# Forget gates in 384-byte rows, joint decay sums and dummy matmuls in a tuned attention-and-feed-forward kernel

## The chip, the cores and the metric

The kernel runs on one core of one Trainium2 chip. The metric is device time in microseconds (us) for one launch, on that core. A run's span is the time from its first to its last instruction; the reported time is some 2 us longer. A run that is more than 1.5% above the fastest run of the same kernel is called slow, and ratios leave it out.

## The reference

The first layer is a gated linear attention with a state of 48 x 48 per head; the second is a feed-forward layer with the activation h + sin²(αh)/α.

```python
# q, k, v, f_logit: (4 batches, 8 heads, 768 tokens, 48)
f = 1.0 / (1.0 + np.exp(-f_logit))
for t in range(S):
    state = f[:, :, t, :, None] * state + np.einsum('bhd,bhe->bhde', k[:, :, t], v[:, :, t])
    y[:, :, t] = np.einsum('bhd,bhde->bhe', q[:, :, t], state)
x = y.transpose(0, 2, 1, 3).reshape(3072, 384)
h = x @ w_in                       # 384 x 2048
s = np.sin(alpha * h)
out = (h + s * s / (alpha + 1e-09)) @ w_out    # 2048 x 384
```

## The kernel before

Tokens are cut into six chunks of 128, and the four batches into two pairs. A pair in a chunk is a **unit**, so there are 12 units, and each needs one load of f, k, q and v (384 KB each). For a unit the kernel takes ln(1 + exp(-f)), sums it over the tokens of the chunk with a triangular mask on TensorE (the **decay sums**, tile `cs`), and multiplies q and k by exponentials of these sums.

A scheduler in the program places every operation. It works from hand-tuned tables of ranks and estimated durations; changing a table or a duration changes the order on every engine. The parts that the change touches:

```python
N_H, N_A, NQ, NV = 3, 3, 6, 4        # N_A: three PSUM banks shared by sums, transposes, scores, values
...
LOADS = [("v", 0), ("f", 0), ("q", 0), ("k", 0), ("f", 1), ("v", 1), ...]   # order in the load queue
W_GATE = [5, 5, 18]                  # w_in's two halves wait for load 5 (counted from 0), w_out for load 18
PHASES = [("pre", [0]), ("pre", [1]), ("sin", 16), ("pre", [2, 3]), ("sin", 16), ("pre", [4, 5]), ...]
...
def emit(e):                          # one load: 128 tokens on 128 partitions, rows of 48 floats (192 B)
    engine[e].dma_start(out=t, in_=srcs[n][bp * 2 * H:(bp + 1) * 2 * H, c * C:(c + 1) * C, :]
                        .rearrange("b c d -> c b d"))
...
def weights_after(i, rank):           # GpSimd reads one number of that load, then issues the weights' DMAs
    u, n = LOADS[W_GATE[i]][1], LOADS[W_GATE[i]][0]
    return op(rank, {POOL: 100}, lambda e: nc.gpsimd.tensor_copy(seen[:, i:i + 1], tl[n, u][0:1, 0, 0:1]), ...)
...
def cs_(e, i=i, m=m):                 # decay sums of ONE batch, in one bank
    cs = tl["cs", m] = ps_a.tile([P, 512], F32, tag="a", name=f"cs_{m}")
    nc.tensor.matmul(cs[:, :H * D]..., mask, lf_b[lf.place % 2][:, :, i, :, :D], start=True, stop=True)
    for p in range(0 if last else HP):
        nc.tensor.matmul(cs[:, H * D + p:H * D + p + 1], lf_b[...][:, p, i, :, :]..., ones_c, ...)
```

A phase `("pre", [2, 3])` runs the exponentials and logarithms of units 2 and 3 interleaved, under one function table of ScalarE; `("sin", 16)` runs sixteen sines under another, and each change of phase loads a table. Below, a **hidden product** is a matmul of x with w_in and an **output product** one with w_out; a **bank** is one of the parts of PSUM, where TensorE's results go; a **spread** is a 16 KB DMA that copies a part of x, transposed (xT), to other partitions.

## Time and profile before

| | before |
|---|---|
| time, median of 3 | 225.85 us (225.22 to 225.99) |
| span of the profiled run | 223.8 us |
| TensorE busy | 186.9 us (84%) |
| VectorE, ScalarE busy | 171.2 us, 160.9 us |
| mean granted TensorE clock | 0.954 |
| packets of the hardware load queue | 111,648 |

No engine is full over the whole span. TensorE is full in the second half and has gaps and a low clock in the first quarter; the prediction shows the slices and stretches from which this is read. ScalarE's table loads divide the front half into blocks, so they serve as milestones (start, length in us, engine, line, operation):

```profile
36.64 1.28 ACT L660 ACT_TABLE_LOAD   x1
45.68 1.28 ACT L660 ACT_TABLE_LOAD   x1
62.14 1.28 ACT L660 ACT_TABLE_LOAD   x1
```

The first sixteen sines end at 36.64; units 2 and 3 are prepared together until 45.68; the next sixteen sines end at 62.14.

### The profile page before, as it was taken

The numbers are of one execution on the slowest core, as the hardware profiler recorded it, in microseconds if no ns is written. First come the engines' busy times: TensorE is split into PE (matmuls) and PEld (weight loads), VectorE is DVE, ScalarE is ACT, GpSimd is POOL, SyncE is SP. The second block draws the span as 40 slices with busy tenths as digits, with TensorE's granted clock in tenths as the row PEclk, the third lists the DMA queues.
The fourth block names the chain that finished last, engine by engine and source line by source line (L and its number), as shares of the span: only waits on it lengthen the run. The fifth ranks groups of instructions, "written<-read, shape, count | busy, mean of one in ns | idle before, by whom it ended". The sixth has DMA issues, their size and how long they took to land.

```text
span 223.8 us, 4257 instructions
## 1 busy us (share of the span) xinstructions
PE 186.9 (84%) x1517; PEld 114.6 (51%) x1517; DVE 171.2 (76%) x306; ACT 160.9 (72%) x260; POOL 117.3 (52%) x142
## 2 busy tenths in 40 slices
PE   0266593848998999969698999988999999999993
PEld 0154382636864555636364655544655555555551
DVE  7769369497895699976997998678999767766730
ACT  2657269874699679978896879998976655688701
POOL 5037559077842696661364564679247778411300
PEclk9999589695899999979999999999999999999999
DMA  8999999995698999979999959966221020100121
GB/s 131 187 186 199 216 202 188 175 201 81 75 147 158 191 168 187 163 185 186 182 212 190 170 75 176 199 136 157 50 45 24 8 83 35 38 35 35 70 73 70
DMA packets 115125, 29.61 MB, mean 132 GB/s; under 512 B 108720, under 2 KB 114336, under 8 KB 115104
## 3 DMA queue, kind: packets, MB, share of 16 engines
q1 hardware_dynamic: 111648, 26.04, 67.4%
q0 software_dynamic: 3456, 3.30, 9.5%
q8 instruction: 12, 0.20, 0.4%
q14 instruction: 9, 0.07, 0.1%
HBM read 25.17 MB, written 4.72 MB: 134 GB/s over the span
## 4 chain that ended last, share of the span: by engine, by line
PE 54%; DVE 15%; ACT 9%; DMA 9%; POOL 5%; SPq 3%; issue 3%; ACTq 0%; POOLq 0%
PE h L549 24%; PE o L597 21%; DVE g L570 6%; SPq L277 3%; PE y L463 3%; DMA w_out_bf<-in_moe_w_out_dram 3%; DMA v<-in_v_dram 3%; DMA w_in_bf<-in_moe_w_in_dram 3%; DVE vb L348 3%; DVE vb L347 3%; ACT s L555 2%; ACT L660 2%; POOL qk L390 2%; DVE at L445 2%; PE aps L442 2%
## 5 line engine op out<-in xcount | busy, mean ns | idle before, releaser
L564 POOL TENSOR_TENSOR s<-s 128x512 f32<-128x512 f32 x63 | 65.5, 1050 | 46.9 <-ACT s L555 38.2
L555 ACT ACTIVATE s<-h,al_p 128x512 f32<-128x512 f32 (+1 forms) x112 | 66.3, 628 | 25.8 <-PE h L549 23.0
L549 PE MATMUL h<-xT,w_in_bf 128*128 128x512 bf16 (+1 forms) x336 | 79.5, 366 | 5.3 <-DMA w_in_bf<-in_moe_w_in_dram 3.4
L570 DVE SCALAR_TENSOR_TENSOR g<-s,al_r,h 128x512 bf16<-128x512 f32 (+1 forms) x112 | 71.1, 665 | 13.4 <-POOL s L564 11.1
L597 PE MATMUL o<-w_out_bf,g 128*128 128x384 bf16 x384 | 77.2, 331 | 2.6 <-DVE osb L605 1.3
L597 PEld LDWEIGHTS <-g 128*128 128x128 bf16 x384 | 36.5, 99 | 28.1 <-issue 3.2
L549 PEld LDWEIGHTS <-w_in_bf 128*128 128x128 bf16 x336 | 33.5, 103 | 29.2 <-DMA w_in_bf<-in_moe_w_in_dram 3.9
L445 DVE TENSOR_TENSOR at<-aps,mask 128x512 bf16<-128x512 f32 x48 | 31.3, 680 | 5.6 <-PE aps L442 5.4
L390 POOL TENSOR_TENSOR qk<-k,Gi 128x384 bf16<-128x384 f32 x20 | 20.5, 1042 | 23.5 <-ACT Gi L381 7.8
L463 PE MATMUL y<-at,vb 128*128 128x128 bf16 x184 | 18.5, 223 | 4.1 <-DVE at L445 2.3
L368 PE MATMUL cs<-lf,mask 128*128 128x384 bf16 x24 | 8.4, 358 | 13.7 <-ACT lf L341 13.5
L390 DVE TENSOR_TENSOR qk<-q,cs 128x384 bf16<-128x384 f32 x24 | 13.2, 549 | 6.9 <-ACT cs L377 6.7
L488 POOL TENSOR_TENSOR st<-sum,gl 128x512 bf16<-128x512 f32 x12 | 12.4, 1043 | 10.6 <-DVE sum L484 10.4
L562 ACT ACTIVATE s<-s 128x512 f32<-128x512 f32 x26 | 16.3, 631 | 0.5
L463 PEld LDWEIGHTS <-vb 128*128 128x128 bf16 x184 | 12.8, 100 | 6.3 <-issue 2.3
L381 ACT ACTIVATE Gi<-cs 128x384 f32<-128x384 f32 x24 | 11.7, 486 | 5.2 <-PE cs L371 5.0
L425 PE MATMUL tp<-ident,qk 128*128 128x128 bf16 x128 | 11.8, 246 | 4.0 <-POOL qk L390 3.5
L470 ACT CAST xT<-y 128x512 bf16<-128x512 f32 (+1 forms) x18 | 10.3, 580 | 6.2 <-PE y L463 5.1
L433 ACT COPY tr<-tp 128x1024 bf16<-128x1024 bf16 x10 | 10.1, 1010 | 6.4 <-PE tp L425 6.4
L660 ACT ACT_TABLE_LOAD x11 | 14.1, 1283 | 0.2
L338 ACT ACTIVATE f<-f 128x768 f32<-128x768 f32 x12 | 10.1, 838 | 5.0 <-DMA f<-in_f_logit_dram 4.9
L425 PEld LDWEIGHTS <-qk 128*128 128x128 bf16 x128 | 9.8, 113 | 6.2 <-POOL qk L390 4.0
(57 smaller groups left out, 178.7 us busy)
## 6 DMA issues: line engine op xcount, KB each, us to landing
v<-in_v_dram SPq DMA_DIRECT2D x12, 384.0 KB, 6.7
f<-in_f_logit_dram SPq DMA_DIRECT2D x12, 384.0 KB, 7.0
q<-in_q_dram SPq DMA_DIRECT2D x12, 384.0 KB, 6.6
k<-in_k_dram SPq DMA_DIRECT2D x12, 384.0 KB, 6.8
out_dram<-osb SPq DMA_DIRECT2D x24, 192.0 KB, 2.1
w_out_bf<-in_moe_w_out_dram POOLq DMA_DIRECT2D x4, 384.0 KB, 6.5
w_in_bf<-in_moe_w_in_dram POOLq DMA_DIRECT2D x8, 128.0 KB, 6.3
w_in_bf<-in_moe_w_in_dram POOLq DMA_DIRECT2D x4, 96.0 KB, 6.1
```

The source lines that it names most:

```text
L390: engine[e].tensor_mul(qk_b[bufs["qk", m].place % NQ][:, "kq".index(n), :, :, :D], tl[n, u][:, i * H:(i + 1) * H, :].rearrange("c (r p) d ...
L425: nc.tensor.transpose(tl[x, "tp"][:, j * HP + p, :], qk_b[qkb.place % NQ][:, j, p, :, :].rearrange("c r e -> c (r e)"), ident)
L445: nc.vector.tensor_mul(tl[x, "at", r], tl[x, "a"][r], mask4)
L463: nc.tensor.matmul(tl[x, "y"][:, blk, :], v_, tl[x, "at", r][:, p, :], start=(first and p == r == 0), stop=(r == 1), skip_group_check=True)
L488: engine[e].tensor_tensor(t, tl[x, "kv"] if c < SUM else tl[x, "sum"], tl["gl", m].unsqueeze(3).to_broadcast([P, HP, 2, E]), Alu.mult)
L549: nc.tensor.matmul(tl[x, "h"][:, part[i]], w_in_bf[:, kb, fbs[i] * P:(fbs[i] + 1) * P], tl["xT", c][:, kb, ts], start=(kb == 0), stop=(kb ...
L555: nc.scalar.activation(out=tl[x, "s"][:, part[i]], in_=tl[x, "h"][:, part[i]], func=Act.Sin, scale=al_p[:, fbs[i]:fbs[i] + 1])
L562: nc.scalar.activation(out=s2, in_=s, func=Act.Square)
L564: engine[e].tensor_mul(s2, s, s)
L570: nc.vector.scalar_tensor_tensor(tl["g", c, fb][:, ts], tl[x, "s2"][:, part[i]], al_r[:, fb:fb + 1], tl[x, "h"][:, part[i]], Alu.mult, Alu ...
L597: nc.tensor.matmul(tl["o", c, t], tl["g", c, fb][:, t * P:(t + 1) * P], w_out_bf[:, fb, :], start=(fb == 0), stop=(fb == FB - 1))
L660: nc.scalar.preload_act_table_set(now)
```

## The change

The intent: fewer and longer DMA rows for the forget gates, so that the saturated first 50 us carry less; fewer small operations on VectorE, by summing both batches of a unit together; dummy matmuls in TensorE's known gaps, so that its clock stays up. The tables are retuned for it.

```diff
+FILL = (12000, 60000)
-LOADS = [("v", 0), ("f", 0), ("q", 0), ("k", 0), ("f", 1), ("v", 1), ("q", 1), ("k", 1), ("v", 2),
+LOADS = [("f", 0), ("v", 1), ("k", 0), ("q", 0), ("q", 1), ("f", 1), ("v", 0), ("k", 1), ("f", 2),
+    ("f", 5), ("v", 3), ...
-W_GATE = [5, 5, 18]
+W_GATE = [7, 9, 17]
-PHASES = [("pre", [0]), ("pre", [1]), ("sin", 16), ("pre", [2, 3]), ("sin", 16), ("pre", [4, 5]), ...
+PHASES = [("pre", [0]), ("pre", [1]), ("sin", 16), ("pre", [2]), ("sin", 6), ("pre", [3]), ("sin", 10),
+    ("pre", [4, 5]), ...
  ... LAG, ATT, RANK, KIND, ON_ACT, BIAS: every number retuned (cut)
+            if n == "f":      # partition = a pair of tokens of one batch; 64 partitions per DMA
+                for i in range(2):
+                    engine[e].dma_start(out=t[i * E:(i + 1) * E].rearrange("c (h s) d -> c h (s d)", s=2),
+                                        in_=f_logit[2 * bp + i, :, c * C:(c + 1) * C, :]
+                                        .rearrange("h (c s) d -> c h (s d)", s=2))
+                return
-        o = bufs[n, u].ready = op(rank, {SP: 500}, emit, takes=[bufs[n, u]], dma=2100)
+        o = bufs[n, u].ready = op(rank, {SP: 1000 if n == "f" else 500}, emit, takes=[bufs[n, u]],
+                                   dma=1400 if n == "f" else 2100)
+        def cs_(e):           # both batches: two banks taken at once
+            cs = [ps_a.tile([P, 512], F32, tag="a", name=f"cs_{2 * u + i}") for i in range(2)]
+            warm(cs[0])
+            for s in range(2):
+                for i in range(2):      # batch i lies on 64 partitions, the other batch on the other 64
+                    nc.tensor.matmul(cs[i][...], maskf[i * E:(i + 1) * E, s, :],
+                                     lft[i * E:(i + 1) * E, :, s, :, :D], start=(s == 0), stop=(s == 1))
+            for p in range(0 if last else HP):
+                for s in range(2):
+                    nc.tensor.matmul(cs[0][:, H * D + 2 * p:H * D + 2 * p + 2], lft[:, p, s, :, :]...,
+                                     in_half, start=(s == 0), stop=(s == 1))
  ... one product gl per unit in place of two (cut)
+    def warm(t):              # dummies, before sums, transposes, scores and the first of a hidden block
+        for _ in range(gaps[0]):
+            nc.tensor.matmul(t, ident, mask4.rearrange("c p x -> c (p x)"), start=True, stop=True)
  ...
+        if e == PE:           # as many as fit in a gap that no bank limits
+            gap = o.start - max(pe_end, o.bank)
+            gaps[0] = max(0, int((gap - min(1500, 200 + gap // 4)) // 220)) if FILL[0] < o.start < FILL[1] else 0
+            pe_end = o.end
```

## The prediction

> **What bounds the kernel now.** I read the page first (busy shares and slices), then stretches of five and more microseconds, then TensorE's own timeline with its waits, and last the chain of waits. The busy shares name no engine: TensorE 84%, VectorE 76%, ScalarE 72%. The slices do: full speed and full occupancy in the second half, gaps and a low clock in the first quarter.
>
> ```profile
> PE   0266593848998999969698999988999999999993
> PEclk9999589695899999979999999999999999999999
> DMA  8999999995698999979999959966221020100121
> ```
>
> A slice is 5.6 us. Until 60 us TensorE is rarely full, and four slices have a clock of 0.5 to 0.8; DMA is saturated until 50 us. The same by stretches (columns: PE, PEld, DVE, ACT, POOL busy with counts, then clock, DMA share, GB/s):
>
> ```profile
> 20.00:25.00 5.00, 1.41 (x18) 0.83 (x14) 2.60 (x6) 3.26 (x4) 2.51 (x5) 0.80 1.17 211
> 25.00:30.00 5.00, 4.73 (x38) 3.75 (x39) 1.98 (x3) 2.27 (x5) 2.19 (x5) 0.52 1.15 211
> ...
> 35.00:40.00 5.00, 0.92 (x12) 0.63 (x11) 5.00 (x13) 4.94 (x9) 3.87 (x4) 1.00 1.34 188
> 40.00:45.00 5.00, 4.48 (x38) 3.18 (x34) 2.02 (x8) 4.19 (x9) 0.69 (x1) 0.66 1.21 175
> ...
> 50.00:55.00 5.00, 4.00 (x25) 3.01 (x26) 4.46 (x9) 1.58 (x4) 3.59 (x4) 0.53 0.75 104
> 55.00:60.00 5.00, 5.00 (x55) 4.12 (x54) 3.31 (x7) 3.53 (x8) 4.30 (x6) 0.79 0.27 29
> 60.00:125.00 65.00, 58.29 (x541) 35.91 (x540) 54.80 (x98) 54.48 (x85) 35.39 (x38) 0.97 1.09 176
> ```
>
> The reader is to see that each stretch of low clock follows one in which TensorE stood nearly idle (1.41 of 5, then 0.92 of 5, then 2.61 in 45 to 50). From 60 us on TensorE is 90% busy, 95% in 125 to 160 and 99% in 160 to 211: there its backlog sets the end. So what the front half saves counts as far as it lets TensorE start that backlog earlier. Its waits in the front, from its timeline (start, length, line, then the idle time before):
>
> ```profile
> 8.80 0.48 PE L368 MATMUL cs<-lf,mask 128*128 128x384 bf16 x1 [8.80 <-ACT lf L341]
> ...
> 12.47 1.03 PE L425 MATMUL tp<-ident,qk 128*128 128x128 bf16 x8 [2.37 <-POOL qk L390]
> ...
> 23.83 0.37 PE L549 MATMUL h<-xT,w_in_bf 128*128 128x256 bf16 x1 [2.38 <-DMA w_in_bf<-in_moe_w_in_dram]
> 25.25 0.39 PE L549 MATMUL h<-xT,w_in_bf 128*128 128x256 bf16 x1 [1.04 <-DMA w_in_bf<-in_moe_w_in_dram]
> ...
> 39.70 0.32 PE L368 MATMUL cs<-lf,mask 128*128 128x384 bf16 x1 [4.08 <-ACT lf L341]
> ```
>
> Two of the waits are for the decay sums' input (the first forget gates, and the exponentials that come after the sine block), one for the weights.
>
> **What the Trainium skill says.** (1) "TensorE: Matmul & The Clock Gate", section "What's actually happening": the clock halves after about one idle window of 3.4 us, and a busy window restores it. The trace agrees in size: three 128x256 matmuls take 0.64 us at 28.92 in the chain, while 21 of them take 2.61 us at 33.01, so 0.21 against 0.12 us each. (2) "DMA: Bandwidth & Descriptors", section "Specifications", puts line rate at pieces of 512 B and more. The trace shows 108720 of 115125 packets under 512 B and 187 to 211 GB/s when saturated; 384-byte pieces are still under that mark, so I expect a part of the gain, not a doubling of the rate. (3) "ScalarE: Activation LUTs", section "Step-by-step: what each stage is for", prices a table load at about 2.7 us with the drain; the trace has 1283 ns, which I use.
>
> **The change, part by part.**
>
> Forget gates. A load is now 2 DMAs with 1024 packets in all instead of one with 2048, so 12 loads save 12,288 packets. Loads follow each other every 2.05 us in the queue's view, 384 KB each. If the cost were all per packet, a load would take 1.03 us, if all per byte 2.05; I take 1.4 (an estimate; the scheduler's table in the diff also says 1400 for 2100). That is 0.65 us a load, 3.9 us for the six gates in the saturated first 50 us. The first gate is also now first in the queue. Before, the first v was issued at 0.82 and exp began at 7.03, which is two loads of 2.05 and a latency of about 2.1. With the new order: 0.82 + 1.4 + 2.1 = 4.3, so exp begins 2.7 us earlier. Then k (third) lands at 0.82 + 2.1 + 5.5 = 8.4 and q (fourth) at 10.5; k before, with four loads in front, at 11.1. With 0.55 us for the q product the first transposes run at about 11.3 instead of 12.47, the second gate's exp at about 14 instead of 15.73: about 1.5 us gained by then.
>
> Weights. The gate of w_in moves from the sixth load to the eighth (and, for the remaining half of its DMAs, to the tenth). Before, the gate opened at 15.54 and the last piece needed arrived at 25.25, 9.7 us later. The eighth load lands at about 18, the tenth at about 21 to 22; the four issues behind it take 2.1 us (0.52 each) and 5 us to land: about 28 to 29. So the first hidden matmul may be 3 us later. Against this, all attention of the first chunk but the last score product stands in front of it in the new order, so the sine block should run denser. I count this as 1 us lost net.
>
> Decay sums. 24 matmuls of 128 rows become 48 of 64 rows in alternating halves; 80 column sums stay 80. If the halves overlap, the 8.4 us stay; otherwise up to 24 x 0.16 = 3.8 us more at full clock, spread over the kernel. VectorE drops 10 products of 161 ns, 1.6 us. But a unit takes two of the three shared banks at once, and its first exponential waits for all 12 matmuls: about 0.5 us later per unit, mostly beside other ScalarE work. I count 0.5 us lost.
>
> Dummies. The built program has 21 of 128x512, 14 of them before one decay sum, the one that waited 4.08 us at 39.70. At 216 to 430 ns that block is 3 to 6 us inside a gap. In 20 to 60 us the low clock cost busy time times missing clock: 0.28 + 2.27 + 1.52 + 1.88 + 1.05 = 7.0 us of TensorE time. Only five dummies lie ahead of the hidden matmuls and two before the sums after, because elsewhere a bank limits the gap. I credit half, 3.5 us, and of that two thirds to the end, 2.3 us, since the chain in 25 to 60 us passes through VectorE (g, at and vb pieces) as well as TensorE.
>
> The schedule. Everything is retuned: two more table loads (2 x 1.28 = 2.6 us of ScalarE, as the second pre block is split), four PSUM copies of 1.01 us and four output copies less on ScalarE, which VectorE takes over at 0.69 and 0.55 us; all 30 spreads go to the sync queue, and three more loads now stand before its first wait for the spread. Before, that queue was blocked from 49.7 to 67.5 us while DMA fell to 29 GB/s. Two output tiles now run before the first chunk's hidden layer is done, 32 x 0.162 = 5.2 us of TensorE work put in its idle time. That is worth something only if VectorE, 96% busy in 80 to 100 us, follows. I credit 2.5 us, less 1 for the table loads.
>
> Sum: 1.5 + 2.3 + 1.5 - 1.0 - 0.5 = 3.8 us off 225.85; with some 0.7 us for the relief of DMA after 60 us (six gates of 0.65, mostly hidden), 4.5 us: 221.3.
>
> **Rivals.** First, weights bind: the second gate makes the first hidden matmul start at 29 and the whole sine block slides by 3 us or more, which eats the rest. For it speaks that the chain before passes through w_in; against it, that DMA has less to carry. Time 224 to 227. Second, VectorE takes over: it gets about 2 us more work and stands at 19.2 of 20 us in 80 to 100; then work saved ahead of 60 us becomes idle time of TensorE, and the time is 223 to 225. Third, the dummies and the earlier output matmuls keep the clock full through the front half and the retuned order closes the 12.6 us that TensorE idles after 60 us: all 7 us of clock and some of the idle time come back, 214 to 218. Fourth, two banks taken at once starve the attention: waits of transposes and scores for banks, 226 to 229; three banks with two claimed at once speak for it, the order tuned to that speaks against.
>
> **Range and chances.** 2% is 221.33 us, so my number lies on the border. The second rival and the third pull about equally; a retuned schedule is rarely slower than its predecessor, so slower by 2% (over 230.4) gets little. 80% range 215.5 to 225.8. Faster 0.48, same 0.46, slower 0.06.
>
> **What would show it.** Right: exp of the first gate begins at 4 to 5 us; packets of the hardware queue fall by some 12,000; clock slices below 0.8 shrink from four to one or two; TensorE's backlog phase starts with two output tiles done near 60 us. Wrong: first hidden matmul after 28 us with the sine block ending later than the 36.6 us of before; low clock in 40 to 60 still; more VectorE waits in 60 to 125, where TensorE would be under 58 of 65 us busy.

## The result, and the profile after

The changed kernel took **234.38 us** (median of 4 runs, one of them slow, 232.40 to 236.63), against 225.91 us of the kernel before in the same rounds. The ratio is **1.035** with a 95% interval of 1.025 to 1.046. (A ratio is the mean time of one kernel's fast runs over that of the other's of the same rounds, so it is not quite the ratio of the medians.) The result is right, the program is 3.5% slower, and the prediction was wrong in sign. The profiled run took 233.0 us with a span of 231.3.

A first ledger comes from the page. TensorE was busy 194.9 us and idle 231.3 - 194.9 = 36.4; before, busy 186.9 and idle 36.9. The dummies take 6.3 of the busy time. Time without useful work is therefore 36.4 + 6.3 = 42.7 against 36.9, so 5.8 us more, and useful work took 188.6 against 186.9, so 1.7 us more. The sum is the 7.5 us by which the span grew: TensorE mostly waits longer.

The slices of the changed kernel, 5.8 us each:

```profile
PE   0378469875898999859985998999999999999993
PEclk9999979999799999988996799999999999999999
DMA  6999999999990599977995992483402021100111
```

There are still four slices with a clock under 0.8, though milder ones (0.6 and 0.7; before 0.5, 0.6, 0.5 and 0.7), and they moved: two lie in the front, near 30 and 60 us, and two near 121 to 133 us, where before there was full speed. By stretches (busy us with counts of PE, PEld, DVE, ACT, POOL, then clock, DMA share, GB/s):

```profile
20.00:25.00 5.00, 4.20 (x46) 3.91 (x44) 3.37 (x8) 2.81 (x6) 4.19 (x10) 1.00 1.38 195
25.00:30.00 5.00, 1.45 (x15) 0.61 (x12) 2.51 (x4) 2.04 (x2) 2.40 (x6) 1.00 1.16 210
30.00:35.00 5.00, 3.98 (x28) 2.80 (x28) 2.72 (x5) 1.88 (x5) 2.93 (x5) 0.66 1.23 203
...
40.00:45.00 5.00, 3.84 (x28) 1.64 (x27) 4.62 (x12) 3.79 (x7) 2.69 (x3) 1.00 1.13 176
...
55.00:60.00 5.00, 1.94 (x17) 0.99 (x14) 1.19 (x3) 4.38 (x10) 3.02 (x4) 0.81 1.25 182
60.00:125.00 65.00, 56.66 (x530) 33.67 (x529) 53.62 (x96) 48.86 (x79) 38.74 (x39) 0.95 0.92 149
```

The empty stretch of TensorE was at 20 to 25 us; now it is at 25 to 30, with the low clock one stretch behind it as before. A second one opened at 55 to 60, where TensorE was full. TensorE's own timeline names the waits (start, length, line, idle time before and its end):

```profile
7.26 0.82 PE L392 MATMUL cs<-lf,maskf 64*128 64x384 bf16 x4 [7.26 <-ACT lf L363]
...
31.00 0.39 PE L587 MATMUL h<-xT,w_in_bf 128*128 128x256 bf16 x1 [1.56 <-DMA w_in_bf<-in_moe_w_in_dram]
...
39.50 3.18 PE L239 MATMUL cs<-mask,ident 128*128 128x512 bf16 x14
43.84 0.77 PE L392 MATMUL cs<-lf,maskf 64*128 64x384 bf16 x4 [1.16 <-ACT lf L363]
...
58.63 2.72 PE L635 MATMUL o<-w_out_bf,g 128*128 128x384 bf16 x8 [3.06 <-DMA w_out_bf<-in_moe_w_out_dram]
```

The first sums start 1.54 us earlier (8.80 to 7.26). Then the lead is gone: the first three products with w_in wait one by one for its pieces, and the third comes at 31.00 instead of 25.25. The 14 dummies fill the old gap of 4.08 us, but the sums that they precede run at 43.84 instead of 39.70. At 58.63 an output product stands in front of TensorE's queue and waits 3.06 us for w_out. The gates of w_in on GpSimd show the first delay; before, then after:

```profile
15.54 0.29 POOL L293 COPY seen<-v 1x1 f32<-1x1 f32 x2 [3.13 <-DMA v<-in_v_dram]
```

```profile
20.05 0.17 POOL L315 COPY seen<-k 1x1 f32<-1x1 f32 x1 [8.49 <-DMA k<-in_k_dram]
...
23.08 0.17 POOL L315 COPY seen<-f 1x1 f32<-1x1 f32 x1 [0.76 <-DMA f<-in_f_logit_dram]
```

The table loads of ScalarE, to be held beside those of before:

```profile
40.78 1.28 ACT L703 ACT_TABLE_LOAD   x1
46.74 1.28 ACT L703 ACT_TABLE_LOAD   x1
50.35 1.28 ACT L703 ACT_TABLE_LOAD   x1
57.41 1.28 ACT L703 ACT_TABLE_LOAD   x1
68.89 1.28 ACT L703 ACT_TABLE_LOAD   x1
```

Before, the two units took 45.68 - 36.64 = 9.04 us and one load back, 1.29: 10.33. Now unit 2 takes 5.96, the load back 1.29, unit 3 takes 7.06, the load back 1.29: 15.60. That is 5.27 us more on ScalarE between the same sines. The other terms up to the third block of units: the first sines end 4.14 us later (40.78 for 36.64), and the second sixteen take 2.32 + 10.19 = 12.51 us for 15.17, a gain of 2.66. In sum 4.14 + 5.27 - 2.66 = 6.75, which is 68.89 - 62.14. In this pair of traces the loss is there by 69 us, and the rest of the kernel adds less than a microsecond to it. But being late here is not the same as ending late: a_oldlayout, an experiment below, stands 6.07 us behind at the same table load (68.21) and ends only 3.8 us behind (span 227.6). The changed kernel got nothing back after 69 us; its TensorE ran at half clock from 102.47 to 105.88 and from 122.95 to 129.77 us, where a_oldlayout's kept its full clock. How much of the loss at the end is the late front, and how much that clock, these two traces don't part.

Of the cost of the split, 2.58 are the two extra table loads. Longer waits of the first exponentials for their sums make 1.02 (1.15 and 0.56 for 0.69), and 1.68 are a copy of xT at 54.45 with the wait of 1.10 in front of it; before, such copies stood in the sine block. The groups of the input gate's exponentials, before and after (count, busy us and mean ns, then the idle time before them and what ended it):

```profile
L381 ACT ACTIVATE Gi<-cs 128x384 f32<-128x384 f32 x24 | 11.7, 486 | 5.2 <-PE cs L371 5.0
```

```profile
L424 ACT ACTIVATE Gi<-cs 128x384 f32<-128x384 f32 x24 | 11.7, 487 | 10.2 <-PE cs L397 8.5 <-PE cs L392 1.6
```

The wait doubled, from 5.2 to 10.2 us over the kernel; a_oldlayout shows below that most of the rise goes with the new sums and not with the split. From these readings came the theories for the experiments: the gate of w_in; the place of w_out's first products; the new layout of the forget gates, either its loads or its sums; the two banks taken at once; the dummies. The rivals were each of these against the others.

### The profile page after: what moved, and what is told of

Its sections match the earlier page's. It is cut to its first block, busy times and chain, and to the rows that moved or that the text cites. A ratio compares the mean times of both kernels' runs of the same rounds, so it can differ in the third digit from the quotient of the medians.

```text
span 231.3 us, 4322 instructions
## 1 busy us (share of the span) xinstructions
PE 194.9 (84%) x1562; PEld 114.2 (49%) x1562; DVE 170.7 (74%) x302; ACT 156.1 (68%) x252; POOL 117.2 (51%) x140
## 3 DMA queue, kind: packets, MB, share of 16 engines
q1 hardware_dynamic: 99840, 26.19, 65.0%
## 4 chain that ended last, share of the span: by engine, by line
PE 56%; DMA 13%; SPq 11%; ACT 11%; issue 3%; DVE 2%; POOL 1%; ACTq 0%; DVEq 0%; POOLq 0%
PE o L635 25%; PE h L587 21%; ACT s L593 4%; SPq L298 4%; SPq L565 4%; SPq L294 3%; DMA xT<-xT 3%; DMA w_out_bf<-in_moe_w_out_dram 3%; ACT L703 3%; DMA w_in_bf<-in_moe_w_in_dram 3%; PE y L500 3%; PE aps L479 2%; DMA v<-in_v_dram 2%; DMA f<-in_f_logit_dram 2%; PE tp L461 2%
## 5 line engine op out<-in xcount | busy, mean ns | idle before, releaser
L602 POOL TENSOR_TENSOR s<-s 128x512 f32<-128x512 f32 x65 | 67.2, 1046 | 58.3 <-ACT s L593 52.0
L593 ACT ACTIVATE s<-h,al_p 128x512 f32<-128x512 f32 (+1 forms) x112 | 65.6, 628 | 36.3 <-PE h L587 35.1
L587 PE MATMUL h<-xT,w_in_bf 128*128 128x512 bf16 (+1 forms) x336 | 76.9, 358 | 8.6 <-DVE g L608 4.1
L587 PEld LDWEIGHTS <-w_in_bf 128*128 128x128 bf16 x336 | 32.6, 100 | 33.4 <-issue 8.8
L427 POOL TENSOR_TENSOR qk<-k,Gi 128x384 bf16<-128x384 f32 x22 | 21.9, 1017 | 21.4 <-ACT Gi L424 17.2
L500 PE MATMUL y<-at,vb 128*128 128x128 bf16 x184 | 17.8, 225 | 1.1 <-ACT xT L507 0.6
L424 ACT ACTIVATE Gi<-cs 128x384 f32<-128x384 f32 x24 | 11.7, 487 | 10.2 <-PE cs L397 8.5
L392 PE MATMUL cs<-lf,maskf 64*128 64x384 bf16 x48 | 6.9, 356 | 10.1 <-ACT lf L363 10.1
L507 ACT CAST xT<-y 128x512 bf16<-128x512 f32 (+1 forms) x17 | 9.4, 571 | 5.4 <-PE y L500 4.7
L643 DVE COPY osb<-o 128x384 f32<-128x384 f32 x18 | 9.8, 549 | 4.3 <-PE o L635 4.3
```

Source lines behind the costliest of these rows:

```text
L427: engine[e].tensor_mul(qk_b[bufs["qk", m].place % NQ][:, "kq".index(n), :, :, :D], tl[n, u][:, i * H:(i + 1) * H, :].rearrange("c (r p) d ...
L500: nc.tensor.matmul(tl[x, "y"][:, blk, :], v_, tl[x, "at", r][:, p, :], start=(first and p == r == 0), stop=(r == 1), skip_group_check=True)
L587: nc.tensor.matmul(tl[x, "h"][:, part[i]], w_in_bf[:, kb, fbs[i] * P:(fbs[i] + 1) * P], tl["xT", c][:, kb, ts], start=(kb == 0), stop=(kb ...
L593: nc.scalar.activation(out=tl[x, "s"][:, part[i]], in_=tl[x, "h"][:, part[i]], func=Act.Sin, scale=al_p[:, fbs[i]:fbs[i] + 1])
L602: engine[e].tensor_mul(s2, s, s)
```

## The experiments

Labels that begin with a_ are edits of the changed kernel, with b_ of the kernel before, with c_ mixtures. "Same order" means that the edit was made to the emitted instructions after the scheduler had placed them, and that the instruction streams were compared. 18 kernels ran. The median and range of each run are beside its ratio to the kernel before.

### Parts of the changed kernel undone, same order

**Without the 21 dummies.** `-FILL = (12000, 60000)` / `+FILL = (0, 0)`.

> The changed kernel without its 21 dummy matmuls; order of everything else the same. Theory W (the weights' gate was put too late and the first hidden matmul slides from 25.3 to 31.0 us, the rest follows): the dummies lie in gaps, so 233 to 236 us, perhaps 1 to 2 us more from a colder clock at 40 to 50 us. Theory D (the dummies themselves cost, they hold TensorE when work comes or feed a later throttle at 100 to 160 us): 228 to 231 us, clock at 100 to 160 back at 0.97 or more.

Measured: 235.26 us (232.22 to 238.14), two of four runs slow, so no ratio. The changed kernel's own runs span 232.40 to 236.63, so this tells nothing of the size of the dummies' effect, only that they are not what lost 8 us.

**Both gates of w_in on the sixth load.**

```diff
+READ = [5, 5, 17]
-        return op(..., tl[n, u][0:1, 0, 0:1]), ...
+        rn, ru = LOADS[READ[i]]
+        return op(..., tl[rn, ru][0:1, 0, 0:1]), ...
```

> The changed kernel in the same order, but both gates of w_in look at the sixth load (the second forget gate) instead of the eighth and tenth. Theory W: the gate opens at about 16 instead of 20.1 and 23.1 us, the first hidden matmul is complete by 26 to 27 instead of 31.0 us, the sine block ends about 4 us earlier, and the time falls to 228 to 231 us. Theory V (DMA throughput is what binds, whoever goes first): the loads behind slide by as much, time stays 232 to 235.

Measured: 230.88 us (229.76 to 234.15), ratio 1.025 (1.019 to 1.032). Its timeline of GpSimd and of TensorE:

```profile
17.08 0.17 POOL L317 COPY seen<-f 1x1 f32<-1x1 f32 x1 [5.30 <-ACT f L362]
```

```profile
27.94 0.28 PE L589 MATMUL h<-xT,w_in_bf 128*128 128x256 bf16 x1 [0.98 <-DMA w_in_bf<-in_moe_w_in_dram]
```

The gate opens only when the exponential over that load is done, at 17.08. The third product comes 3.06 us earlier than in the changed kernel, the first sines end at 39.22 instead of 40.78, and the first hidden matmul of the next chunk starts at 75.42 instead of 77.78. So in the front the later gate costs 1.6 to 3.1 us, by the milestone. The time falls by 3.5 us in the medians and by 1.0% in the ratios, whose intervals overlap. The clock takes part in that: the three fast runs had 0.970 to 0.985, the changed kernel's 0.949 to 0.963, and the one slow run, at 0.956, took 234.15 us, as long as the changed kernel. The smaller gap in front of the weights keeps the clock at 1.00 over 20 to 40 us in the profiled run, where it was 0.91; I can't part the two effects further.

**f as one DMA of 192-byte rows** (wrong on purpose: rows land on other tokens than the sums assume; relative error 0.16). The four-line block for f in the load is deleted.

> The changed kernel in the same order with each forget gate as one DMA of 192-byte rows again (the decay sums then get the wrong tokens: a wrong result on purpose). If 384-byte rows save what I predicted (0.65 us a gate), the eighth load lands 1.3 us later than in the changed kernel and the time rises by 1 to 3 us. If they save nothing, as the equal 186 to 190 GB/s at 8 to 20 us in both traces suggest, the landing of the gates and the time stay within 1 us of the changed kernel's.

Measured: 234.37 us (233.92 to 234.65), ratio 1.042 (1.037 to 1.048). Going back to short rows costs nothing that can be seen. The eighth load was seen by GpSimd at 19.73 instead of 20.05, so the two half DMAs of long rows are no faster than one DMA of short ones.

### The tables

**The changed kernel with all tables of before** (rescheduled).

> The changed code (384-byte rows, joint sums, dummies) with all schedule tables of the kernel before. If the retuned schedule is the loss: 224 to 228 us. If the code parts are the loss (two banks taken at once, first exponential waiting for 12 matmuls, half DMAs): 230 us or more, with idle TensorE in front of decay sums and transposes.

Measured: 252.04 us (251.00 to 252.86), ratio 1.121 (1.115 to 1.127). I read this at first as the price of two banks at once, and made two kernels to split it.

**The new layout with before's tables and durations, no dummies**, either with both banks taken by one operation (c_joint) or one bank per batch (c_split):

```diff
-        c_ = op(..., {PE: 880}, cs_, deps=[l], takes=cbs, holds=[lf])                # c_joint
+            c_ = op(..., {PE: 370}, lambda e, i=i: cs_(e, i), ..., takes=[cb], ...)  # c_split, once per batch
```

> The same as c_split but both batches' banks taken in one operation, as the change does it. If two banks at once are what the old tables cannot bear: 245 us or more, against c_split's 225 to 229. If the 252.0 us came from the new durations of the gate loads in the scheduler's table (1400 for 2100) or from the dummies: within 3 us of c_split.

> All tables and durations of the kernel before, new layout, one bank per batch, order left to the scheduler, no dummies. Should lie near the kernel before, 225 to 229, if the loss of the run with the old tables (252.0 us) comes from taking two banks at once.

Measured: c_joint 253.90 us (252.57 to 254.09), ratio 1.126 (1.121 to 1.130); c_split 234.67 us (231.61 to 236.16, two of four slow), ratio 1.032 (1.025 to 1.039), which misses the 225 to 229 expected. (In c_split, and in a_split below, the sums of a batch also run in a slow form that is explained further down: 13.5 and 14.0 us of TensorE, against 7.3 in c_joint and 6.9 in the changed kernel.) If the joint banks themselves cost 20 us, undoing them in the changed kernel should help:

**The changed kernel and its own tables, but one bank per batch** (rescheduled):

> The changed kernel with its own tables, but each of a unit's two banks for the decay sums taken when its own batch needs it, instead of both at once; rescheduled. With the old tables taking both at once cost 20 us. If the joint taking still costs in the retuned tables: 0.97 to 0.99 of the changed kernel's time, thus 1.005 to 1.025 of the kernel before. If the retuned order has absorbed it: 1.03 to 1.05 of the kernel before; other orders of a schedule tuned for joint banks may also come out worse, over 1.05, and then the run says nothing of the wait itself.

Measured: 253.14 us (251.04 to 254.70), ratio 1.122 (1.112 to 1.131). So taking the banks singly comes out as slow under tables tuned for joint banks as joint banks under tables tuned for single ones, though the slow sums have a part in this run. My theory of the banks fell. I read the three runs near 253 us as tables that fit only the dependencies that they were tuned on; that is an argument, and no run shows it. What joint banks cost a schedule that is tuned for them stays open: no run here isolates it.

### Moves inside the changed kernel's order

**The copy of v for unit 10 moved behind a later product** on VectorE, on top of a_gate6: `+later(made["v", 10], made["g", 1, 12, 0])`. In the changed kernel it waits in front of VectorE's queue:

```profile
98.86 0.45 DVE L369 CAST vb<-v 128x384 bf16<-128x384 f32 x1 [1.64 <-DMA v<-in_v_dram]
```

> The run with the earlier gate of w_in, and one more move: the copy of the tenth unit's v, for which VectorE waits 2.0 us at 94.4 us while four products queue behind it, is placed after the twelfth g product of the second chunk. Theory Q (in-order queues stand before transfers that come later than the schedule's table says): TensorE's wait of 3.3 us at 95 to 98 us shrinks below 1.5 us, and the time falls by 1 to 2.5 us to 228.5 to 230. Rival (TensorE's backlog or ScalarE bind there anyway): within 0.7 us of 230.9.

Measured: 230.62 us (228.17 to 231.28), ratio 1.021 (1.012 to 1.030); TensorE's wait for the hidden products behind it fell from 3.25 to 1.28 us, but 0.3 us in the medians is not resolved.

**The first twelve output products moved behind the transposes of chunk 1, batch 3**, on top of that, so that TensorE doesn't stand before w_out:

```diff
+    last_ = made["tp", 1, 3]
+    for t, fbs in ((0, range(8)), (1, range(4))):
+        for fb in fbs:
+            ... later(made["o", 0, t, fb], last_); last_ = made["o", 0, t, fb]
```

> The former, and the first 12 output matmuls, which stand at 54 to 58 us waiting for w_out (2.2 to 3.1 us) ahead of scores and transposes that need no w_out, are placed behind those transposes. Theory Q: scores start at once, the wait shrinks, the next sine block ends 1.5 to 3 us earlier, 226 to 228.5 us. Rival (the third unit's exponentials and k products bind there, not w_out): within 0.7 us of the former run.

Measured: 228.74 us (228.38 to 229.20), ratio 1.015 (1.007 to 1.023). The wait for w_out is 1.09 us in this run, against 3.06 in the changed kernel:

```profile
59.46 1.78 PE L638 MATMUL o<-w_out_bf,g 128*128 128x384 bf16 x10 [1.09 <-DMA w_out_bf<-in_moe_w_out_dram]
```

But the first hidden matmul of the next chunk is at 75.74, about where it was in a_fix2 (75.98) and a_gate6 (75.42): other waits took the place of the one removed. The two intervals overlap, and its clock was 0.983 to 0.998 in its four runs, against 0.983 to 0.984 in a_fix2. I don't claim the 1.9 us between the two medians for the order alone.

**Half of the xT spreads issued from GpSimd**, as before, on top of a_fix3: `+e = POOL if r else SP`.

> The run with the three moves (gate of w_in, the copy of v, the output matmuls), and of the six spreads of each chunk three are issued from GpSimd again, as in the kernel before (the changed kernel issues all six from the sync queue in 3.7 us). Theory Q: the first hidden matmul of each later chunk starts 1 to 2 us earlier where it waits for the spread, 227 to 228.2 us. Rival: hidden behind output matmuls, or GpSimd's products now wait for the spread's input: 228.4 to 230.

Measured: 233.76 us (231.38 to 237.05), ratio 1.034 (1.027 to 1.041). It got worse, from 1.015 to 1.034: an idea from reading the sync queue alone (the block of six spreads at 72.50 takes 4.58 us there) that failed. In its trace the hidden products at 97.35 wait 3.23 us for VectorE, where a_fix3 waits 1.28 at 98.10, and the clock of 80 to 100 us is 0.92 for 1.00. Which of the moved spreads does it stays open.

### Parts of the change alone in the kernel before, same order

**The dummies alone.** 25 by the same rule, 17 of them before the sums of unit 2.

> The kernel before with dummy matmuls alone, by the same rule (25 of them, 17 before the decay sum that waits 4.1 us at 39.7), order of all else the same. If the clock in 20 to 60 us is worth what I predicted: 222.5 to 224 against 224.8 us, with the clock of 40 to 45 us at 1.0 instead of 0.66. If VectorE and the waits set the pace there: within 0.7 us of the kernel before, though the clock rises.

Measured: 224.16 us (20 runs), ratio **0.994** (0.991 to 0.997). The result is right, and this is the one right version that beats both kernels. Its timeline shows the gap filled and little left of the wait of 4.08 us:

```profile
36.38 3.83 PE L239 MATMUL cs<-mask,ident 128*128 128x512 bf16 x16
40.62 0.32 PE L380 MATMUL cs<-lf,mask 128*128 128x384 bf16 x1 [0.41 <-ACT lf L352]
```

The clock in 40 to 60 us rose from 0.74 to 0.91 and over the run from 0.954 to 0.984, and the time fell by 0.6%.

**f as one DMA over 128 partitions with 384-byte rows** (wrong on purpose, relative error 0.16: both halves come from one batch; a correct single DMA needs four dimensions and couldn't be built).

```diff
+            if n == "f":
+                c4 = min(c, NCH - 2)
+                engine[e].dma_start(out=t.rearrange("c (h s) d -> c h (s d)", s=2),
+                                    in_=f_logit[2 * bp, :, c4 * C:(c4 + 2) * C, :].rearrange("h (c s) d -> c h (s d)", s=2))
+                return
```

> The kernel before, each forget gate loaded as one DMA of 384-byte rows over all 128 partitions (tokens of one batch only: a wrong result on purpose), order the same. If the row length saves and only the halving into two DMAs of 64 partitions ate it: queue spacing of a gate 1.4 instead of 2.05 us, time 0.5 to 2 us under the kernel before. If bytes bind and not rows: spacing 2.0 us, GB/s still 186 to 190, time within 0.7 us.

Measured: 223.34 us (222.00 to 225.46), ratio 0.989 (0.980 to 0.997). Long rows do pay here, by three fast runs, and the third product with w_in comes at 23.50 for 25.25.

**The two half DMAs of 384-byte rows alone** (wrong on purpose), and **two half DMAs of 192-byte rows** (right):

> The kernel before in its exact order, with its own decay sums, but f loaded as two DMAs of 64 partitions with 384-byte rows (wrong on purpose: half of the columns that the sums read are of another token). One DMA of 128 partitions with such rows gave 0.989 of the time before. If it is the halving that eats the gain of the longer rows: ratio 0.998 to 1.012, first w_in product of a whole hidden block near 26.0 us (23.50 with one DMA), and no window of 4 to 6 us above 210 GB/s. If the longer rows pay in halves too: 0.985 to 0.993 and 23.5 to 24.2 us.

> The kernel before in its exact order with f loaded as two DMAs of 64 partitions with 192-byte rows, everything else untouched and the result right. If a 64-partition DMA takes as long as half of a 128-partition one: 0.998 to 1.004. If halving itself costs, as the theory of the halves says: 1.010 to 1.030, with w_in later by 1 to 3 us.

Measured: 225.82 us (20 runs), ratio 1.003 (1.000 to 1.005); and 226.86 us (225.36 to 228.17), ratio 1.004 (1.000 to 1.008). By the time, halving short rows missed its expectation of 1.010 to 1.030. The ninth load's issue on the sync queue tells more, in one trace each, since two gate loads and six others stand before it in each. In the order before, one DMA of long rows, two halves of long rows, two halves of short rows:

```profile
15.03 2.00 SPq L277 DMA_DIRECT2D v<-in_v_dram  x1
```

```profile
13.89 2.00 SPq L282 DMA_DIRECT2D v<-in_v_dram  x1
```

```profile
14.89 2.05 SPq L283 DMA_DIRECT2D v<-in_v_dram  x1
```

```profile
15.70 2.05 SPq L282 DMA_DIRECT2D v<-in_v_dram  x1
```

Long rows in one DMA save (15.03 - 13.89) / 2 = 0.57 us a gate. In halves they save 0.07. Halving short rows costs 0.33. The sixth load, with two gates in it, says the same by its landing: GpSimd saw it at 15.54, 14.40, 15.42 and 16.18. So halving eats what the length gains.

**The whole layout** (half DMAs and 64-row sums, one bank per batch, no dummies; right), and **the 64-row sums alone** (wrong on purpose):

```diff
-                nc.tensor.matmul(cs[...], mask, lf_b[...][:, :, i, :, :D], start=True, stop=True)
+                for s in range(2):
+                    nc.tensor.matmul(cs[...], maskf[i * E:(i + 1) * E, s, :],
+                                     lft[i * E:(i + 1) * E, :, s, :, :D], start=(s == 0), stop=(s == 1))
```

> The kernel before in its exact order, with the new layout of forget gates (two DMAs of 64 partitions, 384-byte rows, sums of 64 rows, column sums of both batches in the first batch's bank), but a bank taken per batch, no dummies: correct result. If halving eats what the rows save: 224.5 to 225.7, queue spacing of a gate 2.0 us or more. If the rows save even so: 223 to 224.3, as with one DMA of 384-byte rows. If the layout itself costs (64-row matmuls, wait of the first exponential): 226 or more.

> The kernel before in its exact order with the single 192-byte-row DMA of f, but the new decay sums of 64 rows and the joint column sums (wrong on purpose: rows land on other tokens than the sums assume). b_newlayout, which has the sums and the halved loads, was at 1.024. If the sums cost most of it: 1.014 to 1.025, and the first exponential of the input gate again about 1.2 us after its logarithm. If the halved loads cost most of it: 1.000 to 1.008.

Measured: 230.27 us (229.44 to 232.56), ratio 1.024 (1.017 to 1.030); and 229.72 us (227.70 to 231.28), ratio 1.016 (1.009 to 1.023). I took this for the layout's price until I held the groups of the sums beside each other: before, b_newlayout, and the changed kernel (count, busy us and mean ns, idle before):

```profile
L368 PE MATMUL cs<-lf,mask 128*128 128x384 bf16 x24 | 8.4, 358 | 13.7 <-ACT lf L341 13.5 <-ACT xT L470 0.2
```

```profile
L380 PE MATMUL cs<-lf,maskf 64*128 64x384 bf16 x48 | 13.7, 371 | 13.9 <-ACT lf L351 13.7 <-DVE at L463 0.2
```

```profile
L392 PE MATMUL cs<-lf,maskf 64*128 64x384 bf16 x48 | 6.9, 356 | 10.1 <-ACT lf L363 10.1
```

The same 48 matmuls take 13.7 us when the two of a batch follow each other on the same 64 rows, and 6.9 us when they alternate between the halves, as the changed kernel has them. My experiment had a cost of 5.3 us that the changed kernel doesn't have. So these two runs don't measure the layout in the changed kernel, and I used the last two to undo the layout where it stands:

**The changed kernel in its order with the old layout** (one DMA, 128-row sums, still two banks at once and dummies; right), and **the same in a_fix3**:

```diff
-            for s in range(2):
-                for i in range(2):
-                    nc.tensor.matmul(cs[i][...], maskf[i * E:(i + 1) * E, s, :], lft[i * E:(i + 1) * E, :, s, :, :D], ...)
+            for i in range(2):
+                nc.tensor.matmul(cs[i][...], mask, lft[:, :, i, :, :D], start=True, stop=True)
+                for p in range(0 if last else HP):
+                    nc.tensor.matmul(cs[0][:, H * D + 2 * p + i:H * D + 2 * p + i + 1], lft[:, p, i, :, :]..., ones_c, ...)
```

> The changed kernel in its exact order, with its dummies and both banks of a unit taken together, but f loaded as before (one DMA of 192-byte rows) and the sums of 128 rows of before; the result stays right. b_newlayout put the layout at +2.4%, but there the two 64-row halves of a batch's sum stood on the same rows one after the other and took 13.7 us of TensorE instead of the 6.9 us in the changed kernel, where they alternate. If the layout costs in the changed kernel too: 1.010 to 1.022 of the kernel before. If it is the order alone that lost the time, and the layout in its overlapping form is free or a small gain: 1.028 to 1.045.

> The same undoing of the layout in a_fix3 (gate on the sixth load, v copy later, twelve output products behind the transposes), which stood at 1.0146 with the new layout. If the layout costs its 2%: 0.990 to 1.000, which would beat both kernels. If it is free: 1.010 to 1.020, and the rest of the loss sits in the retuned order with its joint banks.

Measured: a_oldlayout 230.79 us (229.38 to 233.93, one of six slow), ratio 1.024 (1.018 to 1.031); a_fix3_oldlayout 228.98 us (227.50 to 232.94, two of six slow), ratio 1.012 (1.006 to 1.019). The second pair shows no cost of the layout (1.012 against 1.015), within intervals of some 0.7% to either side. The first lies between the two expectations. The traces say more: the same hidden product in the changed kernel and in a_oldlayout, and two windows of the clock around it:

```profile
100.89 0.81 PE L587 MATMUL h<-xT,w_in_bf 128*128 128x512 bf16 x3 [2.96 <-DVE g L608]
```

```profile
99.06:102.47 3.41, 1.58 (x17) 0.66 (x17) 2.97 (x7) 2.55 (x4) 2.25 (x4) 1.00 0.35 63
102.47:105.88 3.41, 3.41 (x11) 1.43 (x10) 2.43 (x6) 1.73 (x4) 2.74 (x3) 0.50 1.05 275
```

```profile
100.92 0.81 PE L574 MATMUL h<-xT,w_in_bf 128*128 128x512 bf16 x3 [2.96 <-DVE g L595]
```

```profile
99.09:102.50 3.41, 1.58 (x16) 0.96 (x16) 2.97 (x7) 2.76 (x4) 2.25 (x4) 1.00 0.20 38
102.50:105.91 3.41, 3.04 (x25) 1.68 (x24) 1.75 (x5) 2.33 (x6) 2.76 (x3) 1.00 1.04 261
```

At 101 us the two kernels stand within 0.03 us of each other, after the same gap of 2.96 us. Undoing the layout has brought nothing up to there. Then the clock parts them: it fell to half at 102.47 in one profiled run and stayed at 1.00 in the other. The Trainium skill says in "TensorE: Matmul & The Clock Gate", section "What's actually happening", that the clock is decided in windows of about 3.4 us that run free. The traces agree with the length: in the changed kernel's the clock changes at 58.09, 61.51, 102.47, 105.88, 122.95 and 129.77 us, whole multiples of 3.41 us apart. But the place of the window doesn't explain this pair, since the windows lie at 99.06 and at 99.09, and TensorE was busy for 1.58 of 3.41 us in both. What tipped the clock stays open; one difference inside the window is that the sums are of 64 rows in the changed kernel and of 128 rows in a_oldlayout. One caution: the product at 100.9 waits, through VectorE, for the load of v of unit 10 at 98.86 and 98.72, and that wait can hide smaller differences ahead of it; the first hidden product of the next chunk was 0.78 us earlier without the layout (77.00 for 77.78).

The old sums also shorten the waits of the input gate's exponentials, in the same order with its split phases:

```profile
L411 ACT ACTIVATE Gi<-cs 128x384 f32<-128x384 f32 x24 | 11.7, 487 | 7.1 <-PE cs L384 5.8 <-PE cs L381 1.1
```

So 3.1 of the 5.0 us that this wait grew by go with the new sums, and 1.9 with the order; b_newlayout, with the order of before and the new sums in their slow form, also has 10.2. What this idle time of ScalarE costs at the end is not shown. A further pair bears on it: a_rows192 (1.037 to 1.048) has the new sums with the old load, and a_oldlayout (1.018 to 1.031) the old sums with the old load. Those intervals don't overlap, so in this order the new sums cost something, though the clock has a part in that too: in a_rows192's trace it fell twice after 100 us, for 6.8 us each, in a_oldlayout's never. In the front, by the table load at 68.21 in a_oldlayout, the new sums with the old load cost 1.46 us (69.67 in a_rows192) and the whole layout 0.68 (68.89 in the changed kernel). What the layout costs at the end lies between nothing (the pair of a_fix3) and some 2%, and no run settles it. The other 6.07 us of the front belong to the order, late gate included, which a_oldlayout keeps.

## Why the prediction was wrong

Its sum was 4.5 us of gain. Of the signs that it named for being wrong, two came: the first hidden product at 28.05 with the sines ending at 40.78, and TensorE busy for 56.66 of 65 us from 60 to 125. Term by term:

**Gate loads, "I take 1.4 (an estimate ...)".** This step failed. Packets fell by 11,808 (111,648 to 99,840), as predicted, but time did not. Two half DMAs save 0.07 us a gate, not 0.65. For one DMA over 128 partitions the figure was near, 2.05 - 0.57 = 1.48; as it was set between two limits with no measurement behind it, that is in part luck. The Trainium skill has the warning in "DMA: Bandwidth & Descriptors", section "Rules for kernel authors": two transfers to disjoint partition halves serialize, and one transfer over 128 partitions is to be used. I read the page for the row length and missed this line. b_halves192 agrees that halves are no gain, and adds that they cost. The first exponential did start earlier, at 5.49 (predicted 4.3, before 7.03), since its load is first in the queue; with one DMA of short rows in that place it started at 4.91 (a_rows192). The first transposes kept part of the lead (10.67 for 12.47). The second gate, now the sixth load instead of the fifth, was predicted to reach its exponential at about 14 and came at 15.96, later than the 15.73 of before. So by then the term of 1.5 is gone, and with it the ground for the 0.7 of later relief.

**Weights, "I count this as 1 us lost net".** The mechanism was right and described in the first rival; the size was wrong. I predicted the first hidden products up to 3 us later and then set denser sines against it. They came 5.75 us later (the third at 31.00 for 25.25), the first sines ended 4.14 us later, and nothing was denser: TensorE stood at 1.45 of 5 us in 25 to 30. Part of the error came from the term above: the eighth and tenth loads were predicted at 18 and 21 to 22 with the saving of the gates counted in, and were seen at 20.05 and 23.08. Undoing the gate alone brings 1.6 to 3.1 us of the front back (a_gate6).

**Decay sums, "0.5 us lost".** On TensorE the alternating halves do overlap: 6.9 us for 8.4. On ScalarE the waits for sums grew by 5.0 us over the kernel. That is near the 0.5 us per unit that were predicted (6 us for twelve), but it is idle time of ScalarE and not "mostly beside other ScalarE work": the overlap was wrong, not the size. With the old sums in the same order 1.9 us of it are left (a_oldlayout), so most goes with the new sums.

**Dummies, "2.3 us".** Right in sign, mis-sized: 0.6% in the kernel before (224.16 for 224.97, 0.8 us in the medians, 1.3 by the ratio), and not resolved in the changed kernel. The clock of 40 to 60 us did rise, to 0.95 from 0.74, but the gap is also time on the other engines. The prediction let each low clock follow a stretch in which TensorE stood "nearly idle"; 2.61 of 5 us in 45 to 50 is half busy, and before the fall at 50.32 TensorE was busy for 1.48 of 3.42 us.

**The schedule, "I credit 2.5 us, less 1".** This is the step that, by the traces, turned the sign: in place of a gain, 4.7 to 5.0 us of lateness at the third block of units are left when the gate is undone and both moves are made (66.85 in a_fix3, 67.12 in a_fix3_oldlayout, for 62.14). The two output tiles that I called worth something stood in front of TensorE at 58.63 and waited for w_out. The two table loads that I priced at 2.6 us came with the loss of interleaving, 5.27 us together, and made the largest single term in the ledger of ScalarE's milestones. That ledger is read from one trace; no run joined units 2 and 3 again in the new order, so it is an argument from the trace and not shown by experiment. I had taken a retuned table as evidence that it was better, "a retuned schedule is rarely slower than its predecessor", with no reading behind it. The tables were tuned on durations such as 1400 for a gate load that the chip doesn't keep.

Of the 3.5%, undoing the gate of w_in goes with about 1.0%; the two moves in a_fix2 and a_fix3 go with another 1.1%, each with the clock's part in it and with intervals that overlap; and some 1.2% are left in a_fix3_oldlayout, which has neither the late gate nor the new layout, though it still has the dummies that are worth 0.6%. They sit in the order and the joint banks. How they divide between the split phases and the banks stays open. So does the layout's share, which depends on the order around it: undoing it took 1.1% off in the changed kernel and 0.2% in a_fix3.

## What to carry to other kernels

Longer rows are worth having only if the load stays one DMA over all partitions; count packets and measure the queue's spacing, since the first can fall by a tenth with the second unchanged. Before a schedule is credited with anything, mark the same milestones in both orders (first product with the weights, table loads, first use of the second weights) and see which move; tables put to other dependencies than they were tuned for gave kernels 12% slower here, for whatever reason. A milestone is not the end: 6.07 us behind at 68 us became 3.8 at the end in a_oldlayout. When one part of a change is tried alone, check that it runs in the form that it has in the whole: here the same 48 matmuls took 13.7 or 6.9 us by their order.

## What the Trainium skill lacked or had wrong

- "DMA: Bandwidth & Descriptors" says that transfers to partition halves serialize, but gives no cost: two DMAs of 64 partitions in place of one of 128 cost 0.33 us a load of 384 KB with 192-byte rows, and take away 0.50 of the 0.57 us that 384-byte rows save.
- The same page puts line rate at 512 B and more and has no measured rate for rows of 192 or 384 B: with 384-byte rows in one DMA the load took about 1.48 us for 2.05 with 192-byte rows.
- "ScalarE: Activation LUTs" adds a drain to each switch of tables. In this trace the load of 1.28 us at 36.64 is followed by the next exponential at 37.93, with no further gap, so 1.28 us was the whole price of a switch in the queue.
- "TensorE: Matmul & The Clock Gate" lets the clock fall after an idle window of about 3.4 us. Here a window that was far from idle was enough: before the falls at 98.11 in the kernel before and at 102.47 in the changed kernel, TensorE was busy for 1.40 and 1.58 of 3.41 us. The page has no figure for how busy a window must be; the same 1.58 of 3.41 us in a_oldlayout was followed by no fall.
